# Joins of 16-bit halves in four pieces, late half copies over a head, one transfer and the unsplit stores at later steps

## The chip, the cores and the metric

One core of a Trainium2 chip runs the whole program. The metric is device microseconds of one execution; the engines that matter here are TensorE (PE), VectorE (DVE), ScalarE (ACT), GpSimd (POOL) and SyncE (SP), whose queue issues most transfers.

## The reference

Three layers follow one another: bucketed attention, a mixture of experts that sends each token to one of eight experts, and a gated feed-forward layer.

```python
# 2 batches, 8 heads, 768 tokens, head size 64
mask   = q_bucket[:, :, :, None] == k_bucket[:, :, None, :]
scores = np.where(mask, 0.125 * q @ k.T, -1e9)
x      = softmax(scores) @ v                       # to [1536, 512]
# 8 experts, 1536 tokens, width 512, hidden 1024
for e in range(8):
    m = e_idx == e                                 # argmax of x @ w_gate
    h = np.maximum(x[m] @ w1[e], 0)
    out[m] = gate_w[m, None] * eom[m, e, None] * (h @ w2[e])
# 1536 tokens, 512 -> 1536 -> 512
return ((out @ w_a) * (out @ w_b)) @ w_out
```

## The kernel before

The order of the instructions on each engine is the order of the code (a manual schedule); nothing reorders them.

**Precision.** Every fp32 operand of a matmul is split into a high part (ACT copies it to the narrower type) and a low part (DVE or POOL subtracts), and three matmuls replace one. `w_split` (L510, L511) does this for the weights of the experts, `x_parts` (L961, L962) for their inputs, `mm1` (L978, L979) for the hidden values `hl`.

**Attention**, 16 heads of six blocks of 128 queries, counted as (head, block). `smax` (L166, L167) ends with a small DVE instruction, `sb`, whose result ACT's exponential needs; PE then transposes the result (L188). The attention output `x_b` is kept in fp32 for the router and also written as two planes of 16-bit halves, `x_q` (POOL, `late_planes`, L224), because rows are sent to their expert's slots by POOL's indirect transfers (`scatter`, L454) and come back by a transposing transfer that takes 16-bit elements only. Expert 0's rows of batch 0 are fetched earlier by plain transfers and joined by `x0_join` (L409).

**Experts.** A step (e, f) is expert e with the hidden slice f of 128, 64 steps in all. In a step PE runs `mm1(e, f)` (12 matmuls) and then `mm2` of the step before (8 matmuls, L1005 and L1006); ACT and DVE make `hl` of the step, split the weights of two slots further on, and do what the schedule adds: `y_sum` at f = 0, `y_store` at f = 1 (high parts by ACT, L1029, low parts by DVE, L1030, unsplit copies by ACT, L1032). After each split SP issues the next load into the same buffer (`w_load`, four buffers for each half of a slot). `x_load(e)` is the transposing transfer of expert e's rows (L948, on SP), `x_join(e)` puts the two halves of its elements together again (POOL, L952), `x_parts` then splits them in two halves, i = 0 and 1. For expert 1 the load is issued ahead of step (0, 0), the join at (0, 5), the parts at (0, 6) and (0, 7). For a later expert the load is at f = 6 two experts ahead, the join at f = 3 and the parts at f = 4 and 6 of the expert before.

POOL also clears `y_h`, `y_l` and `y_w` (L851, four instructions for each), and at every third step from (1, 1) to (5, 2) sends one group of token numbers (`id_scatter`, L454). Ahead of each of these it reads one column of the step's `hl` (`spare`, L1091), so that it starts only after DVE has made `hl`. `hl` has three buffers: the value of step n + 3 can be written only when all readers of step n's are done.

Of the kernel before, what the change touches and what calls it, by code (L numbers as in the profile page):

```python
# [7 lines left out]
F32 = mybir.dt.float32  # L8
# [4 lines left out]
U16 = mybir.dt.uint16  # L13
# [11 lines left out]
C = 224  # L25
# [9 lines left out]
def attn_moe_kernel(ctx: ExitStack, tc: tile.TileContext, xin, cst, projd, wblk, wmoe, w2in, out):  # L35
    nc = tc.nc
    PE, ACT, DVE, POOL = nc.tensor, nc.scalar, nc.vector, nc.gpsimd
# [180 lines left out]
    def halves(ap):  # L218

        return ap.bitcast(U16).rearrange("p t (n a) -> p t a n", a=2)  # L220
# [5 lines left out]
    def late_planes(hh, t0=0, nt=6):  # L226
        to_planes(t0, nt, hh, halves(x_b)[:, t0:t0 + nt, :, hh * 64:(hh + 1) * 64])
# [177 lines left out]
    def x0_join():  # L405
        x0["g"] = xp.tile([128, 2, DM], F32, tag="x", name="x0")
        q = x0.pop("q").bitcast(U16).rearrange("p c (a n) -> p c a n", a=2)
        for c in range(2):
            POOL.tensor_copy(halves(x0["g"])[:, c], q[:, c])  # L409

    def x0_first(lo, hi):
        if lo == 0:
# [219 lines left out]
    with tc.manual_schedule():  # L632
# [80 lines left out]
        for g in range(NG):  # L713
# [75 lines left out]
            if h and h < L and t == 5 and K["avl"].count(5):  # L789
                o_evac(h - 1)  # L790
            side(2)
            if h == L - 2 and t > 2:
                late_planes(t - 3)
            for f in extra.get((h - L + 1, t), ()):
                f()
        o_out(L, qa)
# [48 lines left out]
        y_l = yp.tile([128, 4, N + C], F32R, name="y_l")  # L845
        y_w = yp.tile([128, 4, N + C], F32, name="y_w")

        def y_clear(*ys):
            for y in ys:
                for d in range(4):  # L850
                    POOL.memset(y[:, d], 0.0)  # L851

        y_clear(y_h.bitcast(F32))
        r2 = ctx_2.enter_context(tc.tile_pool(name="r2", bufs=2, reuse_waits="tile"))
        c2 = ctx_2.enter_context(tc.tile_pool(name="c2", bufs=2, reuse_waits="tile"))
        s2 = ctx_2.enter_context(tc.tile_pool(name="s2", bufs=4, reuse_waits="tile"))
# [90 lines left out]
            XG[e] = xg.tile([128, 8, C], U16, tag="xg", name="xg")  # L947
            after(nc.sync.dma_start(out=XG[e], in_=x_rows[e * C:(e + 1) * C], transpose=True), scat_x)  # L948

        def x_join(e):  # L950
            XI[e] = xg.tile([128, 4, C], F32, tag="xi", name="xi", bufs=1)
            POOL.tensor_copy(  # L952
                XI[e].bitcast(U16).rearrange("p d (n a) -> p a d n", a=2), XG.pop(e).rearrange("p (a d) n -> p a d n", a=2)
            )

        def x_parts(e, i):
# [68 lines left out]
        def y_store(e):  # L1025
            sl = bass.ds(o_regs[e], C)
            for d in range(4):
                y = YS[e, d]
                ACT.activation(y_h[:, d, sl], y, ACTF.Copy)  # L1029
                DVE.tensor_tensor(out=y_l[:, d, sl], in0=y, in1=y_h.bitcast(F32)[:, d, sl], op=ALU.subtract)  # L1030
            for d in range(4):
                ACT.activation(y_w[:, d, sl], YS.pop((e, d)), ACTF.Copy)  # L1032

# [28 lines left out]
            (7, 7): [ids_load, lambda: s_work(1, 1), lambda: s_work(1, 2)],  # L1062
        }
        steps = [(e, f) for e in range(E) for f in range(8)]
        x_load(1)
        for n, (e, f) in enumerate(steps):
            mm1(e, f)
            if n:
                mm2(*steps[n - 1])
            if f == 0 and e:  # L1070
                y_sum(e - 1)
            w_split(n + 2, 0)
            w_split(n + 1, 1)
            if f == 1 and e:
                y_store(e - 1)
            if e + 1 < E:
                if f == (3 if e else 5):
                    x_join(e + 1)
                for i in range(2):
                    if f == ((4, 6) if e else (6, 7))[i]:  # L1080
                        x_parts(e + 1, i)
            if (e, f) == (0, 5):
                y_clear(y_l.bitcast(F32), y_w)
            if f == 6 and e + 2 < E:
                x_load(e + 2)
            if e == E - 4 and f in (2, 4):
                w2_load(f // 2 - 1)
            for g in pre2.get((e, f), ()):
                g()
            if 9 <= n < 45 and n % 3 == 0:  # L1090
                POOL.tensor_copy(spare, HT[e, f].bitcast(F32)[:, 1, 0:1])  # L1091
                id_scatter(n // 3 - 3)
            if f == 0 and e or (e, f) == steps[-1]:
                offset_load(e - (f == 0))
# [363 lines left out]
```

## Time and profile before

| | |
|---|---|
| median of three runs | 737.4 us (736.58 to 739.29) |
| the profiled execution's own time | 735.29 us |
| its span, first to last instruction | 733.5 us |
| PE busy | 707.1 us, 96% of the span |
| DVE, ACT, POOL busy | 567.8, 447.4, 260.1 us |
| mean granted TensorE clock | 0.996 of full speed |

The span is the time from the first to the last instruction of the program on the profiled core; 1.8 us of the execution lie outside it. Busy shares are means over three stages: attention runs to about 260 us, the experts to about 441 us, the last layer to the end.

### The profile page before, as it was taken

To read this page: it belongs to the slowest core of one execution; us is meant where nothing else is said; L and a number is where in the kernel's file an instruction comes from. 1 tells how busy PE (TensorE), PEld (TensorE's weight loads), DVE (VectorE), ACT (ScalarE), POOL (GpSimd) and SP (SyncE) were. 2 spreads that over 40 slices of the span, in tenths; PEclk is the share of its full clock that TensorE was granted. 3 is DMA by queue.
4 is the path that set the end of the run, shared out by engine and by line. 5 is a ranking of instruction groups with operands and counts; after the bars stand their busy time and mean duration, and the time that the engine had idled before them with its cause. 6 is when DMAs were issued, how large, how long until landed. Compare 5 with 4: busy or idle time off the path is not lost.

```text
span 733.5 us, 13070 instructions
## 1 busy us (share of the span) xinstructions
PE 707.1 (96%) x4505; PEld 603.9 (82%) x4506; DVE 567.8 (77%) x1102; ACT 447.4 (61%) x962; POOL 260.1 (35%) x262
## 2 busy tenths in 40 slices
PE   7899999999999998899999999999999999999995
PEld 5676677667756688899899899999999999999994
DVE  6778777888787778788889887877777777777644
ACT  6878777777776447477778776576344454434320
POOL 3243343333545469232322103234322332233224
PEclk9999999999999999999999999999999999999999
DMA  7357351221301048579798740132212212121013
GB/s 254 106 216 262 102 171 59 88 87 59 135 15 62 15 131 267 172 224 222 209 281 240 238 139 30 57 109 71 80 53 64 87 58 86 35 82 59 0 51 126
DMA packets 53432, 88.01 MB, mean 120 GB/s; under 512 B 19872, under 2 KB 23280, under 8 KB 53360
## 3 DMA queue, kind: packets, MB, share of 16 engines
q1 hardware_dynamic: 50688, 80.61, 36.1%
q0 software_dynamic: 2304, 6.31, 2.3%
q8 instruction: 37, 0.61, 0.4%
q14 instruction: 35, 0.29, 0.1%
q10 hardware_dynamic: 368, 0.20, 0.1%
HBM read 69.65 MB, written 13.12 MB: 113 GB/s over the span
## 4 chain that ended last, share of the span: by engine, by line
PE 82%; DVE 5%; POOL 4%; ACT 3%; issue 2%; DMA 2%; ACTq 0%; SPq 0%; DVEq 0%; POOLq 0%
PE tp L188 9%; PE av L203 8%; PE y L1005 5%; PE s L160 4%; PE s L161 4%; PE aba L1227 4%; PE abb L1227 4%; PE abb L1229 3%; PE aba L1229 3%; PE abb L1228 3%; PE aba L1228 3%; PE q L1157 3%; PE q L1158 3%; PE q L1156 3%; PE h L967 3%; PE h L965 3%
## 5 line engine op out<-in xcount | busy, mean ns | idle before, releaser
L166 DVE TENSOR_REDUCE mm<-s 128x1 f32<-128x768 f32 x96 | 91.0, 948 | 25.2 <-PE s L161 24.7
L175 ACT ACTIVATE p<-s,sb 128x768 f32<-128x768 f32 x96 | 95.0, 989 | 24.1 <-DVE sb L167 23.0
L188 PEld LDWEIGHTS tp<-cs,p 128*128 128x128 f32 x576 | 64.1, 140 | 38.4 <-ACT p L175 25.1
L511 DVE TENSOR_TENSOR wl<-wr,wh 128x512 fp32r<-128x512 f32 x125 | 89.4, 755 | 6.1 <-ACT wh L510 1.3
L188 PE MATMUL tp<-cs,p 128*128 128x128 f32 x576 | 82.2, 279 | 6.2 <-ACT p L175 3.0
L938 POOL TENSOR_TENSOR pc<-t,pc 128x256 fp32r<-128x256 f32 x38 | 32.8, 867 | 152.8 <-ACT pc L937 138.1
L192 ACT ACTIVATE pt<-tp 128x384 f32<-128x384 f32 x143 | 65.0, 487 | 31.0 <-PE tp L188 31.0
L1005 PE MATMUL y<-hl,wh 128*128 128x448 f32 x224 | 75.8, 381 | 6.5 <-DVE hl L979 6.5
L510 ACT ACTIVATE wh<-wr 128x512 fp32r<-128x512 f32 x128 | 73.6, 623 | 2.7 <-DMA wr<-wmoe 2.7
L160 PE MATMUL s<-tk,tq 76*128 76x384 f32 x192 | 73.1, 381 | 0.5 <-DVE tq L137 0.5
L967 PE MATMUL h<-xh,wl 128*128 128x224 f32 x256 | 71.0, 278 | 1.5 <-DVE wl L511 1.5
L966 PE MATMUL h<-xl,wh 128*128 128x224 f32 x256 | 70.6, 276 | 0.8 <-DVE xl L962 0.5
L965 PE MATMUL h<-xh,wh 128*128 128x224 f32 x256 | 70.8, 276 | 0.2 <-ACT xh L444 0.2
L203 PE MATMUL av<-pt,v 128*64 128x384 f32 x360 | 68.0, 499 | 0.2 <-DVE r L238 0.2
L161 PE MATMUL s<-bk,bq 128*128 128x384 f32 x192 | 65.1, 339 | 0.0
L1006 PE MATMUL y<-hl,wl 128*128 128x224 f32 x224 | 59.9, 267 | 0.0
L1005 PEld LDWEIGHTS y<-hl,wh 128*128 128x128 f32 x224 | 42.6, 190 | 10.6 <-DVE hl L979 7.5
L967 PEld LDWEIGHTS h<-xh,wl 128*128 128x128 f32 x256 | 49.5, 193 | 1.7 <-DVE wl L511 1.7
L965 PEld LDWEIGHTS h<-xh,wh 128*128 128x128 f32 x256 | 49.3, 193 | 1.7 <-ACT xh L444 0.4
L966 PEld LDWEIGHTS h<-xl,wh 128*128 128x128 f32 x256 | 49.5, 193 | 1.2 <-DVE xl L962 0.7
L888 ACT ACTIVATE x<-r 128x512 uint8<-128x512 uint8 x36 | 28.5, 791 | 35.3 <-DVE x L885 35.3
L1117 ACT ACTIVATE gh<-p 128x384 fp32r<-128x384 f32 x21 | 11.0, 525 | 63.5 <-DVE p L1246 62.0
(260 smaller groups left out, 1940.5 us busy)
## 6 DMA issues: line engine op xcount, KB each, us to landing
wr<-wmoe SPq DMA_DIRECT2D x128, 256.0 KB
r<-w2in SPq DMA_DIRECT2D x36, 512.0 KB
x<-xin SPq DMA_DIRECT2D x30, 384.0 KB
xr<-zero SPq DMA_DIRECT2D x13, 512.0 KB
v<-xin SPq DMA_DIRECT2D x16, 192.0 KB
wb<-wblk SPq DMA_DIRECT2D x1, 640.0 KB
x<-xin SPq DMA_DIRECT2D x3, 192.0 KB
tq<-code SPq DMA_DIRECT2D x30, 18.0 KB
```

Of the source, the lines that this page charges most:

```text
L160: PE.matmul(p[:, c, :384], T[h, 0][:76, qs], T[h, 1][:76, sl], start=True, stop=False)
L161: PE.matmul(p[:, c, :384], B[h, 0][:, qs], B[h, 1][:, sl], start=False, stop=True)
L166: DVE.tensor_reduce(out=m[:, 1:2], in_=st[g][:, :, :384], axis=AX.XY, op=ALU.min)
L175: ACT.activation(p.rearrange("p (c n) -> p c n", c=2), st.pop(g)[:, :, :384], ACTF.Exp, scale=scl.pop(g), bias=nbs.pop(g), accum_out=sums[ ...
L188: PE.transpose(ps[:, j * 128:(j + 1) * 128], pt_[g][:, k * 128:(k + 1) * 128], ident)
L203: PE.matmul(av[h][c * 64:(c + 1) * 64, :384], v, PT[h][:, k, c * 384:(c + 1) * 384], start=(k == 0), stop=(k == NT - 1), skip_group_check= ...
L510: ACT.activation(h, r, ACTF.Copy)
L511: eng.tensor_tensor(out=l, in0=r, in1=h.bitcast(F32), op=ALU.subtract)
L965: PE.matmul(ps, wh, xh, start=first, stop=False)
L966: PE.matmul(ps, wh, xl, start=False, stop=False)
L967: PE.matmul(ps, wl, xh, start=False, stop=last)
L1005: PE.matmul(p, wh[:, w], hl, start=(f == 0), stop=False, skip_group_check=True)
```

## The change

`x0_join` and `x_join` are cut into four pieces each. The pieces of `x0_join` follow one another as before. Those of `x_join` go to the steps f = 1, 2, 4, 5 (for expert 1, two at (0, 4) and two at (0, 5)), and for expert 2 and the later ones each of them stands behind a `spare` copy of its step's `hl`. The three copies of `late_planes` that stood at blocks 3, 4 and 5 of head 13 go to blocks 1, 3 and 4 of head 14, each behind a one-column copy (`held`) of the newest `sb`. `x_load(1)` moves from ahead of step (0, 0) to (0, 3). Half of the clearing of `y_h` moves behind pieces of expert 1's join. The unsplit copies leave `y_store` and become `y_keep`, at f = 2 (at f = 4 for expert 0's result).

```diff
--- before.py
+++ after.py
@@ -406,7 +406,8 @@
         x0["g"] = xp.tile([128, 2, DM], F32, tag="x", name="x0")
         q = x0.pop("q").bitcast(U16).rearrange("p c (a n) -> p c a n", a=2)
         for c in range(2):
-            POOL.tensor_copy(halves(x0["g"])[:, c], q[:, c])
+            for w in (slice(0, 256), slice(256, 512)):
+                POOL.tensor_copy(halves(x0["g"])[:, c, :, w], q[:, c, :, w])
 
     def x0_first(lo, hi):
         if lo == 0:
@@ -789,8 +790,9 @@
             if h and h < L and t == 5 and K["avl"].count(5):
                 o_evac(h - 1)
             side(2)
-            if h == L - 2 and t > 2:
-                late_planes(t - 3)
+            if h == L - 1 and t in (1, 3, 4):
+                POOL.tensor_copy(held, last[0])
+                late_planes((1, 3, 4).index(t))
             for f in extra.get((h - L + 1, t), ()):
                 f()
         o_out(L, qa)
@@ -845,12 +847,11 @@
         y_l = yp.tile([128, 4, N + C], F32R, name="y_l")
         y_w = yp.tile([128, 4, N + C], F32, name="y_w")
 
-        def y_clear(*ys):
-            for y in ys:
-                for d in range(4):
-                    POOL.memset(y[:, d], 0.0)
-
-        y_clear(y_h.bitcast(F32))
+        def y_clear(y, ds=range(4)):
+            for d in ds:
+                POOL.memset(y[:, d], 0.0)
+
+        y_clear(y_h.bitcast(F32), (0, 1))
         r2 = ctx_2.enter_context(tc.tile_pool(name="r2", bufs=2, reuse_waits="tile"))
         c2 = ctx_2.enter_context(tc.tile_pool(name="c2", bufs=2, reuse_waits="tile"))
         s2 = ctx_2.enter_context(tc.tile_pool(name="s2", bufs=4, reuse_waits="tile"))
@@ -947,10 +948,12 @@
             XG[e] = xg.tile([128, 8, C], U16, tag="xg", name="xg")
             after(nc.sync.dma_start(out=XG[e], in_=x_rows[e * C:(e + 1) * C], transpose=True), scat_x)
 
-        def x_join(e):
-            XI[e] = xg.tile([128, 4, C], F32, tag="xi", name="xi", bufs=1)
+        def x_join(e, d):
+            if e not in XI:
+                XI[e] = xg.tile([128, 4, C], F32, tag="xi", name="xi", bufs=1)
             POOL.tensor_copy(
-                XI[e].bitcast(U16).rearrange("p d (n a) -> p a d n", a=2), XG.pop(e).rearrange("p (a d) n -> p a d n", a=2)
+                XI[e].bitcast(U16)[:, d].rearrange("p (n a) -> p a n", a=2),
+                XG[e].rearrange("p (a d) n -> p a d n", a=2)[:, :, d],
             )
 
         def x_parts(e, i):
@@ -1028,6 +1031,9 @@
                 y = YS[e, d]
                 ACT.activation(y_h[:, d, sl], y, ACTF.Copy)
                 DVE.tensor_tensor(out=y_l[:, d, sl], in0=y, in1=y_h.bitcast(F32)[:, d, sl], op=ALU.subtract)
+
+        def y_keep(e):
+            sl = bass.ds(o_regs[e], C)
             for d in range(4):
                 ACT.activation(y_w[:, d, sl], YS.pop((e, d)), ACTF.Copy)
 
@@ -1062,7 +1068,6 @@
             (7, 7): [ids_load, lambda: s_work(1, 1), lambda: s_work(1, 2)],
         }
         steps = [(e, f) for e in range(E) for f in range(8)]
-        x_load(1)
         for n, (e, f) in enumerate(steps):
             mm1(e, f)
             if n:
@@ -1073,14 +1078,25 @@
             w_split(n + 1, 1)
             if f == 1 and e:
                 y_store(e - 1)
+            if f == (4 if e == 1 else 2) and e:
+                y_keep(e - 1)
+            if (e, f) == (0, 3):
+                x_load(1)
             if e + 1 < E:
-                if f == (3 if e else 5):
-                    x_join(e + 1)
+                for d in range(4):
+                    if f == ((1, 2, 4, 5)[d] if e else 4 + d // 2):
+                        if e:
+                            POOL.tensor_copy(spare, HT[e, f].bitcast(F32)[:, 1, 0:1])
+                        x_join(e + 1, d)
                 for i in range(2):
                     if f == ((4, 6) if e else (6, 7))[i]:
                         x_parts(e + 1, i)
+            if (e, f) == (0, 4):
+                y_clear(y_h.bitcast(F32), (2,))
             if (e, f) == (0, 5):
-                y_clear(y_l.bitcast(F32), y_w)
+                y_clear(y_h.bitcast(F32), (3,))
+                y_clear(y_l.bitcast(F32))
+                y_clear(y_w)
             if f == 6 and e + 2 < E:
                 x_load(e + 2)
             if e == E - 4 and f in (2, 4):
```

On POOL, from the last row scatter of the router to expert 2's join (`xi` is the joined input, `xg` the transposed rows, `idtab` the token numbers), this stood in a row before:

```order
L454 DMA xr<-x_q,pos_i 3328x512 x6
L851 MEMSET y_h 128x1760 x4
L952 COPY xi<-xg 128x2x896
L851 MEMSET y_l 128x1760 x4
L851 MEMSET y_w 128x1760 x4
L1091 COPY spare<-hl 128x1
L454 DMA idtab<-tokc,cpos_i 1536x2
L952 COPY xi<-xg 128x2x896
```

and this stands there now:

```order
L455 DMA xr<-x_q,pos_i 3328x512 x6
L852 MEMSET y_h 128x1760 x2
L954 COPY xi<-xg 128x2x224 x2
L852 MEMSET y_h 128x1760
L954 COPY xi<-xg 128x2x224 x2
L852 MEMSET y_h 128x1760
L852 MEMSET y_l 128x1760 x4
L852 MEMSET y_w 128x1760 x4
L1089 COPY spare<-hl 128x1
L954 COPY xi<-xg 128x2x224
L1107 COPY spare<-hl 128x1
L455 DMA idtab<-tokc,cpos_i 1536x2
```

The whole join of expert 1 stood ahead of eight of the twelve clearing instructions; its first two pieces stand ahead of ten of them and the other two ahead of nine. The next expert's join has become pieces, each behind a `spare` copy of its own.

On SP, from the loads of the first weights (`wr`) on, this stood in a row before:

```order
L403 DMA x0q<-xr 128x512 x2
L501 DMA wr_2860<-wmoe 128x512
L501 DMA wr_2866<-wmoe 128x512
L501 DMA wr_3059<-wmoe 128x512
L948 DMA_TRANSPOSE xg<-xr 128x8x224
L501 DMA wr_3384<-wmoe 128x512
L501 DMA wr_3390<-wmoe 128x512
```

and this stands there now:

```order
L502 DMA wr_3385<-wmoe 128x512
L502 DMA wr_3391<-wmoe 128x512
L502 DMA wr_3425<-wmoe 128x512
L502 DMA wr_3431<-wmoe 128x512
L502 DMA wr_3468<-wmoe 128x512
L502 DMA wr_3474<-wmoe 128x512
L502 DMA wr_3524<-wmoe 128x512
L502 DMA wr_3530<-wmoe 128x512
L949 DMA_TRANSPOSE xg<-xr 128x8x224
L502 DMA wr_3567<-wmoe 128x512
```

The transposing transfer has moved behind eight weight loads, those of steps (0, 0) to (0, 3).

On ACT, at (7, 1) and (7, 2), where expert 6's result is stored, the end of the stores was this before:

```order
L1029 ISA
L1029 ACTIVATE y_h<-yt 128x224
L1032 ISA
L1032 ACTIVATE y_w<-yt 128x224
L1032 ISA
L1032 ACTIVATE y_w<-yt 128x224
L1032 ISA
L1032 ACTIVATE y_w<-yt 128x224
L1032 ISA
L1032 ACTIVATE y_w<-yt 128x224
L978 ACTIVATE hl<-h_5870 128x224
```

and is this now:

```order
L1032 ISA
L1032 ACTIVATE y_h<-yt 128x224
L981 ACTIVATE hl<-h_5916 128x224
L511 ACTIVATE wh_5944<-wr_5757 128x512
L511 ACTIVATE wh_5948<-wr_5763 128x512
L1038 ISA
L1038 ACTIVATE y_w<-yt 128x224
```

The next step's `hl` and weights have moved ahead of the four unsplit copies. On DVE and PE nothing changes its place.

## Rows read from the trace of the kernel before

**Rows 1.** PE's waits over the span: us in total, times, longest.

```profile
PE y L1005 <- DVE hl L979: 6.5, 5, 2.5
```

**Rows 2.** Engines by stretch: length; PE, PEld, DVE, ACT, POOL busy; clock; DMA; GB/s.

```profile
310.45:313.06 2.61, 2.61 (x22) 2.53 (x21) 1.87 (x5) 1.45 (x5) 1.28 (x2) 1.00 1.04 250
...
277.06:281.46 4.40, 2.86 (x22) 2.61 (x21) 4.33 (x8) 2.67 (x7) 4.40 (x4) 1.00 0.89 314
284.07:287.73 3.66, 3.12 (x22) 2.69 (x21) 2.83 (x10) 1.85 (x6) 3.66 (x4) 1.00 0.95 240
293.00:302.61 9.61, 7.08 (x43) 6.68 (x41) 7.17 (x12) 3.61 (x9) 3.03 (x3) 0.82 0.51 162
297.48:300.88 3.40, 3.40 (x17) 3.27 (x15) 2.20 (x5) 0.00 (x0) 0.00 (x0) 0.50 0.62 186
360.10:364.43 4.33, 2.87 (x23) 2.62 (x21) 4.33 (x8) 2.69 (x7) 1.79 (x1) 1.00 0.34 123
403.63:408.19 4.56, 2.85 (x22) 2.60 (x21) 4.56 (x9) 3.07 (x8) 1.16 (x1) 1.00 0.45 165
423.94:430.34 6.40, 6.08 (x50) 5.58 (x49) 4.59 (x12) 6.31 (x18) 0.00 (x0) 1.00 0.80 246
```

**Rows 3.** Timeline of DVE at (2, 1), where POOL joins nothing.

```profile
316.88 1.29 DVE L1030 TENSOR_TENSOR y_l<-yt,y_h 128x224 f32 x4
318.51 0.39 DVE L979 SCALAR_TENSOR_TENSOR hl<-h,hl 128x224 fp32r<-128x224 f32 x1 [0.34 <-ACT hl L978]
```

**Rows 4.** Timeline of DVE and POOL at step (1, 1): start, us, instruction.

```profile
293.01 3.06 DVE L1030 TENSOR_TENSOR y_l<-yt,y_h 128x224 f32 x1
...
292.39 1.26 POOL L454 DMA_INDIRECT idtab<-tokc,cpos_i  x1 [0.15 <-issue]
293.65 2.21 POOL L952 COPY xi<-xg 128x1792 uint16<-128x1792 uint16 x1
```

**Rows 5.** Timeline of SP and POOL around expert 7's transfer and join.

```profile
395.57 3.57 SPq L948 DMA_TRANSPOSE xg<-xr  x1
...
402.05 2.73 POOL L952 COPY xi<-xg 128x1792 uint16<-128x1792 uint16 x1
```

**Rows 6.** Timeline of ACT, SP and DVE at steps (0, 3) and (0, 4).

```profile
276.05 1.29 ACT L510 ACTIVATE wh<-wr 128x512 fp32r<-128x512 f32 x2 [2.17 <-DMA wr<-wmoe]
...
270.13 1.59 SPq L948 DMA_TRANSPOSE xg<-xr  x1
...
273.15 1.29 DVE L511 TENSOR_TENSOR wl<-wr,wh 128x512 fp32r<-128x512 f32 x2
276.71 2.81 DVE L511 TENSOR_TENSOR wl<-wr,wh 128x512 fp32r<-128x512 f32 x2 [1.30 <-ACT wh L510]
```

**Rows 7.** Timeline of ACT and PE at (7, 1) to (7, 2).

```profile
427.09 1.22 ACT L1032 ACTIVATE y_w<-yt 128x224 f32 x4
...
428.59 0.37 PE L994 MATMUL y<-hl,wh 128*128 128x224 f32 x1 [0.27 <-ACT hl L978]
```

**Rows 8.** Timeline of POOL, DVE and PE at the end of head 13.

```profile
212.58 2.35 POOL L224 COPY x_q<-x_b 128x768 uint16<-128x768 uint16 x3
...
213.22 1.73 DVE L167 SCALAR_TENSOR_TENSOR sb<-mm 128x2 f32<-128x2 f32 x1
...
216.20 0.33 PE L188 MATMUL tp<-cs,p 128*128 128x128 f32 x1 [1.13 <-DVE r L239]
```

**Rows 9.** POOL's column copies ahead of `id_scatter`: count, min/median/max ns, first and last start.

```profile
L1091 POOL COPY spare<-hl x12: 183/186/581, 291.7 to 383.4; 128x1 f32<-128x1 f32 x12
```

**Rows 10.** DMA packets that began between 270.13 and 273.9 us.

```profile
DMA packets 1854, 0.52 MB, mean 138 GB/s; under 512 B 1824, under 2 KB 1824, under 8 KB 1854
```

**Rows 11.** Timeline of POOL behind the last row scatter.

```profile
270.17 6.10 POOL L851 MEMSET y_h<- 128x1760 f32 x4 [2.07 <-DMA xr<-x_q,pos_i]
...
278.35 6.10 POOL L851 MEMSET y_l<- 128x1760 f32 x4
284.39 6.10 POOL L851 MEMSET y_w<- 128x1760 f32 x4
```

## Prediction

> **What bounds the kernel now.** I read the waits of PE first, since PE is busy for nearly the whole span. In the experts' stage its one repeated wait is for the low part of `hl` on DVE: five times, 6.5 us together [rows 1]. A wait of PE understates what is lost, so I took the stage step by step next, in the view of stretches [rows 2]. The first row there is an undisturbed step, 2.61 us from one `mm1` to the next. The reader should see how rarely a step is longer. Outside the first steps behind the router, which the change leaves alone, these are longer: (0, 6) with 4.40 us, 1.79 too much; (1, 0) with 3.66, 1.05 too much; (1, 3) and (1, 4) with 9.61 together, 4.39 too much; (4, 3) with 4.33, 1.72 too much; (6, 3) with 4.56, 1.95 too much. Steps (7, 2) and (7, 3) take 6.40 together, 1.18 more than two undisturbed steps; PE runs slightly longer matmuls in that expert, so I count 1.0. All this is 11.9 us. In the pair at 293 us half of the loss is the clock: PE's granted clock is 0.50 from 297.48 to 300.88 us, the level of 1.2 GHz, after PE had waited for `hl`; at half speed 3.4 us lose 1.7.
>
> Then I looked for what is late in each, in the timelines.
>
> At (1, 1) a `y_l` subtraction, 0.3 us in an undisturbed row of four [rows 3], takes 3.06 us, and it ends when POOL's whole join of 2.21 us ends [rows 4]. The next `hl` stands behind it on DVE, and PE waits for that. (4, 3) and (6, 3) are the same pattern; at (6, 1) the join takes 2.73 [rows 5]. The Trainium skill says the same in GPSIMD Engine Reference, Key points: POOL shares its SBUF interfaces with VectorE, and contends with VectorE instructions that have two SBUF inputs. The trace agrees, with 3.06 against 0.32. By that rule alone the time in which POOL may hold DVE rises, as an estimate, from 6 joins of 2.2 us to 24 pieces with their column copies, 19 us, and the gain at the joins would be in doubt.
>
> At (0, 4) ACT waits 2.17 us for weights [rows 6]. The transposing transfer stands at the head of SP's queue until the row scatters have landed, 270.13, and all weight loads behind it are late. DVE's pair of weight subtractions then takes 2.81 instead of 1.29 beside the join.
>
> At (7, 1) to (7, 2) ACT makes four unsplit copies, 1.22 us, ahead of `hl`, and PE waits for `hl` on ACT [rows 7]. At the end of head 13 three POOL copies in a row, 2.35 us, hold `sb` for 1.73, and PE idles 1.13 us soon after [rows 8].
>
> **The change part by part.**
>
> *Late copies, head 14.* Three copies of 0.78 us leave the place where they hold `sb` for 1.73 us; PE's wait of 1.13 goes. They come back in head 14 with three column copies, which I price like `spare`, 0.19 us each and 0.58 at most [rows 9]. A copy behind `sb` has most of a block's time until the next `sb`, but the last two meet other POOL work of that head. I charge 0.4 (bounds 0, if all fall between two `sb`, and 1.1, if one place waits as today): -0.7. The four pieces of `x0_join` run back to back as its two did; I count nothing, bounds -0.3 and +0.4, since DVE may get in between pieces or wait for all.
>
> *Transfer at (0, 3).* Weight loads no longer wait for the scatters, so the 2.17 us of ACT's wait and the longer subtraction go, and (0, 6) falls to 2.61: -1.8. The transfer itself is now behind the weight loads of step (0, 3), which wait for DVE's subtractions ending at 274.4 [rows 6]; with two issues it starts at about 274.9. Its 1,792 packets of 256 bytes had all begun 3.8 us after the issue [rows 10], which with a little for the landing gives 279.1; expert 7's, in a busier stretch, took 6.5 (395.57 to 402.05 [rows 5]), which gives 281.4. I take 279.1, since the rings are as empty here as at 270.
>
> *Expert 1's join and the clearing.* POOL now idles from 273.2 (two clears of 1.52, a quarter of 6.10 [rows 11]) until 279.1. A piece I put at 0.6 us: 0.55 is a quarter of 2.21, and 0.78 a third of the 2.35 of three larger copies [rows 8]. So: two pieces to 280.3, a clear to 281.8, two pieces to 283.0, a clear to 284.5, `y_l` to 290.6, `y_w` to 296.7; before, all ended at 290.5. PE, without the stall at (0, 6), begins (1, 0) at 277.06 + 2 x 2.61 = 282.3. Today the second parts cost step (1, 0) 1.05 us although the join was done by 278.35 [rows 11]; now ACT comes to them at about 282.4 and finds the last piece 0.6 us later: +0.65, step (1, 0) loses 1.7. (1, 1) begins at 286.6. Its `y_l` subtractions come near 290, when these clears are about done.
>
> *Steps (1, 1) to (1, 5).* The join that held `y_l` for 3.06 us is gone from (1, 1), and with it the slow clock: -4.4. What is late next is POOL. Its first `spare` reads (1, 1)'s `hl` only behind `y_w`, at 296.9; that buffer is wanted by `hl` of (1, 4), which ACT would write at 295.8 and PE needs at 298.3. ACT is 1.1 us late there and PE is not. Then come a piece, a `spare`, the scatter (1.26 us with 0.15 ahead of it [rows 4]), a `spare`, a piece: 299.9, when the first parts of expert 2 can start. ACT has `hl` of (1, 5) behind them, on DVE at 301.4; PE wants it at 300.9. I charge 0.8 in all: -3.6.
>
> *Steps (4, 3) and (6, 3).* A piece of 0.6 us behind `hl` holds one weight subtraction instead of 2.2 us on `y_l`. At (4, 3): -1.7. At (6, 1) the products of the last layer's weights on POOL stay: -1.5 of 1.95.
>
> *Unsplit copies.* For experts 1 to 6 four copies of 1.22 us leave (e, 1), the fullest step of ACT, for (e, 2). That frees `hl` of the next step by 1.2 us, and the loss at (7, 2) goes: -1.0. In the other experts it is not on PE's path: DVE waited for it 0.34 us [rows 3], PE not.
>
> What else moved past what: the clears and the scatter of (1, 1) wait behind the first join on POOL, and only `y_store`, `y_keep` and the list read at the end of the stage want them; SP's later loads wait for 1.6 us of the transfer's issue [rows 6] while their weights are two steps away.
>
> Sum: -0.7 - 1.8 + 0.65 - 3.6 - 1.7 - 1.5 - 1.0 = -9.65; I round to -9.4 for small new waits behind 24 gated pieces. From the profiled execution's 735.29 us this gives 725.9; the median of the three runs is 737.4, 2.1 higher, and the measured median should fall by the same amount: **728.0 us**.
>
> **The rivals.**
>
> *POOL's lateness takes the place of the join (1, 4).* For: 290.5 becomes 296.7 while PE is 5 us earlier, and each microsecond of a later landing counts at (1, 0) and again at (1, 5). Against: three `hl` buffers cover most of it. With 281.4 as the landing, 2.3 us come twice, and PE's wait at (1, 5) reaches the 2.5 us [rows 1] after which the clock was halved, 1.7 more: +6.3, 734.3 at most; a landing half-way gives 732. Chance 0.16.
>
> *The pieces hold DVE as often as they free it.* In (e, 0) and (e, 1) DVE works about 5.9 us against 5.2 of PE (two `hl` of 0.39, two pairs of weight subtractions of 1.29, four `y_l` of 1.29 together [rows 3, 6], and four sums that I put as long), so it ends 0.7 late; `hl` can be ready 0.8 after its matmuls and is wanted a step after them, which leaves 2.61 - 0.8 - 0.7 = 1.1 us. A piece and a column copy are 0.6 + 0.2 and fit; with the longest column copy, 0.58, they pass it by 0.1, and with that of a scatter as well by 0.7. At 0.6 in six experts the gain shrinks by 3.6: 731.6. Against: the gate lets `hl` through first. Chance 0.12. The Trainium skill's rule from GPSIMD Engine Reference speaks for this rival.
>
> *Nothing comes of it.* PE's matmuls may only wait elsewhere, as ACT and DVE stay as busy. Against: the undisturbed step [rows 2] shows PE's own rate with ACT busy 1.45 us and DVE 1.87 of its 2.61, so there is room for what moves. 736, chance 0.07.
>
> *Slower.* One mechanism: the transposing transfer lands late. Nothing else waits on SP's order here, but expert 1 cannot begin without it. The loss is 2 us for each, and two stretches of slow clock, 3.4; against -9.4 the kernel is slower by more than 3.7 from 13.1, that is a landing 4.85 us later than 279.1, at 284 us, 9 us after its issue. The longest in the rows is 6.5. Price at 284.2: 741.5. Chance 0.05.
>
> **How the numbers follow.** The likeliest case has 0.60 and its own range is 725 to 731: lower by 3 where the charges of 0.8, 0.65 and 0.4 vanish and pieces cost nothing, higher by 3 with pieces of 0.78 (0.7 more in the chain, twice) and 1.1 in head 14. The range 724.5 to 734.0 takes in the first two rivals and leaves out the last two and a little below, under 0.2. Under 0.5%, 3.7 us, this kernel's runs can't tell a change from none: the bound of faster is 733.7. That holds the likeliest case and nearly all of the first two rivals, 0.85; the same 0.10; slower 0.05.
>
> **What would show it.** Right: step (0, 6) at 2.61 with no wait of ACT for weights; no `y_l` or weight subtraction on DVE over 1.4 us; (1, 3) and (1, 4) without a stretch at clock 0.50; (4, 3), (6, 3) and (7, 3) near 2.65; head 13 without the wait of 1.13. The terms I trust least show at 279 to 301 us: POOL's start on expert 1's pieces, the end of `y_w`, and PE's waits at (1, 0) and (1, 5). If a slow clock appears there, the first rival holds. If `hl` of (e, 2) still ends PE's waits in several experts, the second does.

## The result, and the profile after

The changed kernel takes **727.57 us** (median of 4 runs, 727.09 to 728.39) where the kernel before took 737.91 (the three runs named at the start and a fourth, 736.58 to 739.29): a ratio of 0.9861, 95% interval 0.9839 to 0.9883, 10.3 us less. The profiled execution takes 728.01 us, its span is 726.3 us, its mean granted clock 0.995. By the two profiled executions only 7.3 us went; the other 3 us are taken up below.

The page's first part, busy time of each engine with its share of the span:

```profile
PE 706.5 (97%) x4505; PEld 604.2 (83%) x4506; DVE 558.9 (77%) x1102; ACT 448.2 (62%) x962; POOL 284.4 (39%) x312
```

POOL does 24 us more (pieces, their column copies), DVE 9 us less, since it is held for less time; PE does the same work in a shorter span. The view of stretches, for the steps that stood in [rows 2] (length; PE, PEld, DVE, ACT, POOL busy; clock; DMA; GB/s):

```profile
275.59:278.19 2.60, 2.60 (x22) 2.53 (x21) 2.31 (x8) 1.45 (x4) 0.60 (x1) 1.00 0.98 215
280.99:288.07 7.08, 4.83 (x20) 4.10 (x21) 5.25 (x12) 3.23 (x8) 7.08 (x7) 0.79 0.80 182
285.13:288.55 3.42, 3.42 (x16) 3.25 (x15) 1.69 (x6) 1.67 (x5) 3.42 (x3) 0.50 0.30 104
293.53:298.75 5.22, 5.22 (x42) 5.07 (x41) 4.02 (x10) 2.32 (x6) 5.06 (x7) 1.00 0.70 226
356.30:358.91 2.61, 2.61 (x23) 2.54 (x21) 2.35 (x7) 2.52 (x8) 2.26 (x3) 1.00 0.77 199
398.01:401.03 3.02, 2.87 (x23) 2.61 (x21) 3.02 (x8) 3.02 (x9) 1.50 (x3) 1.00 0.74 241
416.77:422.59 5.82, 5.82 (x51) 5.51 (x49) 4.46 (x11) 5.72 (x17) 0.00 (x0) 1.00 0.85 253
```

They are (0, 6), (1, 0), the stretch of slow clock, (1, 3) with (1, 4), (4, 3), (6, 3), and (7, 2) with (7, 3). Of the losses named there (6, 3) keeps 0.4 us and the last pair 0.6 (5.82 for two steps of 2.61); the others but one are gone. The exception is (1, 0): 7.08 where 3.66 stood. The slow clock of 297.5 us is gone too, but one of the same length now stands at 285.1 us. Its cause stands in the timelines of SP, POOL, ACT and PE:

```profile
264.44 8.06 SPq L502 DMA_DIRECT2D wr<-wmoe  x8
273.07 2.14 SPq L949 DMA_TRANSPOSE xg<-xr  x1
...
273.11 3.08 POOL L852 MEMSET y_h<- 128x1760 f32 x2 [5.10 <-DMA xr<-x_q,pos_i]
278.35 1.98 POOL L954 COPY xi<-xg 128x448 uint16<-128x448 uint16 x2 [2.16 <-DMA xg<-xr]
280.24 1.57 POOL L852 MEMSET y_h<- 128x1760 f32 x1
281.75 1.73 POOL L954 COPY xi<-xg 128x448 uint16<-128x448 uint16 x2
...
283.51 0.58 ACT L964 ACTIVATE xh<-xi 128x448 fp32r<-128x448 f32 x1 [1.29 <-POOL xi L954]
...
281.65 0.37 PE L969 MATMUL h<-xl,wh 128*128 128x224 f32 x1 [0.29 <-DVE xl L965]
284.14 0.37 PE L968 MATMUL h<-xh,wh 128*128 128x224 f32 x1 [1.67 <-ACT xh L964]
284.80 0.37 PE L969 MATMUL h<-xl,wh 128*128 128x224 f32 x1 [0.29 <-DVE xl L965]
```

The eight weight loads now go out while the row scatters are still under way, so the last scatter lands at about 273.1 us instead of 270.1 [rows 6, 11]: POOL, which waits for it, stands idle 5.10 us behind its issue instead of 2.07. In the four profiles with no load beside the scatters (before, runs 1, 8 and 12) this is 2.06 to 2.07, in the ten others 3.9 to 5.1. The transfer starts then, its rows are there at 278.35, and the pieces of the join take 0.99 and 0.87 us each, not 0.6. The last one ends at 283.48. PE had come to (1, 0) at 280.99 and waits three times.

### The profile page after: what moved, and what is told of

Read it like the earlier page. It is cut to its first block, busy times and chain, and to the rows that moved or that the text cites. A ratio compares the mean times of both kernels' runs of the same rounds, so it can differ in the third digit from the quotient of the medians.

```text
span 726.3 us, 13141 instructions
## 1 busy us (share of the span) xinstructions
PE 706.5 (97%) x4505; PEld 604.2 (83%) x4506; DVE 558.9 (77%) x1102; ACT 448.2 (62%) x962; POOL 284.4 (39%) x312
## 4 chain that ended last, share of the span: by engine, by line
PE 86%; DVE 5%; ACT 3%; DMA 2%; POOL 2%; issue 2%; SPq 0%; DVEq 0%; POOLq 0%; ACTq 0%
PE tp L188 9%; PE av L203 8%; PE y L1008 6%; PE s L160 4%; PE s L161 4%; PE aba L1243 4%; PE abb L1243 4%; PE abb L1245 3%; PE aba L1245 3%; PE abb L1244 3%; PE aba L1244 3%; PE q L1173 3%; PE h L969 3%; PE h L970 3%; PE q L1174 3%; PE h L968 3%
## 5 line engine op out<-in xcount | busy, mean ns | idle before, releaser
L512 DVE TENSOR_TENSOR wl<-wr,wh 128x512 fp32r<-128x512 f32 x125 | 83.5, 708 | 4.2 <-ACT wh L511 0.3
L939 POOL TENSOR_TENSOR pc<-s,pc 128x256 fp32r<-128x256 f32 x44 | 38.0, 874 | 33.0 <-ACT pc L938 31.4
```

The costliest lines, as they stand in the source:

```text
L512: eng.tensor_tensor(out=l, in0=r, in1=h.bitcast(F32), op=ALU.subtract)
```

## Experiments

One number for the first expert's transfer runs through them: by how much the steps exceed 2.61 us each, once from the start of (0, 3) to that of (1, 0), five steps, and once from there to (1, 7), seven steps. It is worked out from the starts of each step's first matmul in the profiled execution: after the change 280.99 - 267.77 - 5 x 2.61 = 0.17.

| kernel | median us | ratio to before | (0, 3) to (1, 0) | (1, 0) to (1, 7) | sum |
|---|---|---|---|---|---|
| before, the profile shown | 737.4 | | 3.16 | 5.49 | 8.7 |
| after | 727.57 | 0.9861 | 0.17 | 4.91 | 5.1 |
| 1 before again | 738.29 | 1.0005 | 6.24 | 3.88 | 10.1 |
| 2 before, transfer at (0, 3) | 736.83 | 0.9993 | 2.17 | 6.56 | 8.7 |
| 3 after, whole join, gated | 730.26 | 0.9902 | 2.17 | 5.98 | 8.2 |
| 4 after, pieces, ungated | 731.11 | 0.9922 | 1.74 | 4.71 | 6.5 |
| 5 after, transfer at (0, 1) | 727.05 | 0.9873 | 1.33 | 2.53 | 3.9 |
| 6 as 5, pieces first | 726.33 | 0.9856 | 1.20 | 2.49 | 3.7 |
| 7 after, pieces first | 728.81 | 0.9888 | 2.48 | 5.25 | 7.7 |
| 8 before, late copies only | 737.29 | 1.0003 | 4.68 | 5.46 | 10.1 |
| 9 as 6, three clears ahead | 726.32 | 0.9843 | 0.02 | 2.94 | 3.0 |
| 10 as 9, transfer at (0, 2) | 726.28 | 0.9849 | -0.02 | 3.11 | 3.1 |
| 11 before, transfer at (0, 1) | 735.69 | 0.9970 | 0.50 | 6.43 | 6.9 |
| 12 before, unsplit copies later | 737.01 | 0.9992 | 6.10 | 3.86 | 10.0 |

Runs 1 to 4, 5 to 8 and 9 to 12 each share their runs of before (medians 737.98, 737.02 and 738.00), so across these groups the ratios compare, not the medians; runs 9 to 12 are from another chip than 1 to 8. The last three columns are of one execution each.

### 1 and 2. The kernel before again, and with the transfer alone moved

Run 1 has no edit. Run 2:

```diff
-        x_load(1)
         for n, (e, f) in enumerate(steps):
...
+            if (e, f) == (0, 3):
+                x_load(1)
```

> The kernel before, unchanged, to see which of its losses belong to every execution. Its profile lost 0.85 and 0.52 us at steps (0, 3) and (0, 4), where ACT stood still from 265.6 to 269.1 us, and these are gone in the changed kernel, which the prediction did not foresee. Theory: the stop comes with the transfer that holds SP's queue at its head, so it stands here again (3.4 to 3.5 and 3.1 us). Rival: it was a stray of one execution, and the two steps take 2.61 here. Both: (0, 6) 4.4, (1, 3) and (1, 4) together 9 to 10 us, (4, 3) 4.3, (6, 3) 4.5; time 737.9, ratio 1.000.

> The kernel before with x_load(1) at (0, 3) and nothing else. Theory: the weights come in time, so (0, 6) falls from 4.40 to 2.61, and (0, 3) and (0, 4) too if their loss hangs on the transfer: -1.8 to -3.2. The whole join, behind all four clears of y_h, ends near 281.5, and the second parts come 1 to 2 us late, so step (1, 0) takes 6 to 7.5 us with a stretch of slow clock in place of 3.66; (1, 3) and (1, 4) keep their 9 to 10. Sum 0 to +1: 737 to 739. Rival: the late load costs expert 1 nothing beyond today's 1.05, and the whole gains 2 to 3: 735.

Measured: 1.0005 [0.9988, 1.0022] and 0.9993 [0.9973, 1.0012]. Stretches of run 1, then of run 2:

```profile
277.79:284.59 6.80, 5.10 (x20) 4.74 (x21) 6.38 (x12) 4.00 (x8) 6.80 (x5) 0.62 0.97 336
279.40:286.20 6.80, 6.23 (x26) 6.06 (x27) 5.41 (x13) 2.88 (x6) 6.80 (x6) 0.50 0.87 299
296.90:304.91 8.01, 5.49 (x43) 5.15 (x41) 7.17 (x12) 3.59 (x9) 3.03 (x3) 1.00 0.48 145
```

```profile
276.49:279.09 2.60, 2.60 (x22) 2.53 (x21) 2.31 (x8) 1.45 (x4) 2.29 (x2) 1.00 1.30 127
279.09:283.33 4.24, 2.77 (x23) 2.44 (x21) 1.16 (x3) 0.96 (x3) 2.86 (x2) 1.00 1.00 332
283.33:289.58 6.25, 5.29 (x21) 4.49 (x21) 4.29 (x12) 3.12 (x8) 6.25 (x5) 0.62 0.74 204
```

Two things follow. First, the profile from which I predicted was not a usual execution. In run 1 step (0, 6) takes 6.80, not 4.40, with 6.8 us at half clock from 279.4; (1, 3) with (1, 4) takes 8.01, not 9.61. Runs 8 and 12, which share the early transfer, agree in the sum: 10.1, 10.1 and 10.0 in the last column against 8.7. Nor did ACT's stop at (0, 3) come again in run 1, both steps took 2.61, so the transfer at the queue's head does not bring it about. Second, the transfer at (0, 3) alone frees (0, 6), 2.60, and gives all of it back at (0, 7) and (1, 0), where the rows come late.

### 3 and 4. The cut without its smallness, and without its gate

Run 3 joins expert 2 and later ones in one instruction again, at f = 3, but behind a `spare`; run 4 keeps the pieces and drops the `spare` ahead of each.

```diff
# run 3; in x_join, d may be a slice there (not shown)
-                    if f == ((1, 2, 4, 5)[d] if e else 4 + d // 2):
+                    if not e and f == 4 + d // 2:
+                        x_join(e + 1, d)
+                if e and f == 3:
+                    POOL.tensor_copy(spare, HT[e, f].bitcast(F32)[:, 1, 0:1])
+                    x_join(e + 1)
# run 4
-                        if e:
-                            POOL.tensor_copy(spare, HT[e, f].bitcast(F32)[:, 1, 0:1])
```

> The changed kernel, but from expert 2 on the join is whole again (2.2 to 2.7 us, one instruction) and stands at f = 3 behind one copy of that step's hl, as the pieces do. Theory of place: the loss came from the step at which the hold fell, (e, 1), DVE's fullest, and ahead of hl; behind hl of (e, 3) DVE ends 1.3 us late of 1.8 that it has, so no step from (1, 3) on is longer than in the changed kernel: 727 to 728.5. Theory of size: a hold of 2.2 us on DVE stops PE wherever it falls: steps (e, 4) lose 0.5 to 1.7 each, six times, +3 to +10: 731 to 738.

> The changed kernel without the copy of hl ahead of each piece of x_join from expert 2 on, so POOL runs a piece as soon as it is free. Theory of place: at (4, 1) and at (6, 1) two pieces, 1.4 us, fall on y_l again and steps (4, 3) and (6, 3) lose 0.3 to 1.7 each: +0.5 to +3, 728 to 730.5. Theory of size: pieces of 0.7 us are short enough anywhere, (4, 3) stays at 2.61 and the time at 727.6.

Measured: 0.9902 [0.9884, 0.9919] and 0.9922 [0.9901, 0.9943]. Run 3, POOL and DVE at (6, 3) and (6, 4), and the stretches (4, 3), (6, 3), (6, 5):

```profile
404.87 0.55 POOL L1091 COPY spare<-hl 128x1 f32<-128x1 f32 x1 [4.29 <-DVE hl L983]
405.36 2.71 POOL L954 COPY xi<-xg 128x1792 uint16<-128x1792 uint16 x1
...
405.89 2.46 DVE L886 TENSOR_SCALAR x<-t 128x512 uint32<-128x512 uint32 x1
...
360.27:362.88 2.61, 2.61 (x22) 2.54 (x21) 1.88 (x5) 2.51 (x8) 0.09 (x1) 1.00 0.98 230
402.09:404.70 2.61, 2.61 (x22) 2.54 (x21) 2.61 (x8) 2.61 (x9) 0.00 (x0) 1.00 0.69 221
407.31:411.20 3.89, 2.87 (x22) 2.62 (x21) 2.72 (x5) 2.82 (x7) 0.76 (x1) 1.00 0.59 178
```

Run 4, POOL, DVE and PE at (6, 1) to (6, 3), and the stretches (4, 3) and (6, 3):

```profile
395.84 1.72 POOL L939 TENSOR_TENSOR pc<-t,pc 128x256 fp32r<-128x256 f32 x2 [12.22 <-ACT pc L938]
397.50 2.99 POOL L954 COPY xi<-xg 128x448 uint16<-128x448 uint16 x3
...
396.86 2.30 DVE L512 TENSOR_TENSOR wl<-wr,wh 128x512 fp32r<-128x512 f32 x2
399.09 2.62 DVE L1033 TENSOR_TENSOR y_l<-yt,y_h 128x224 f32 x4
...
402.07 0.47 PE L1008 MATMUL y<-hl,wh 128*128 128x448 f32 x1 [1.50 <-DVE hl L982]
...
357.36:359.97 2.61, 2.61 (x23) 2.54 (x21) 2.61 (x5) 2.52 (x8) 2.47 (x3) 1.00 0.59 213
399.07:403.42 4.35, 2.85 (x23) 2.61 (x21) 4.35 (x9) 3.08 (x9) 2.15 (x3) 1.00 0.54 186
```

Gate and cut each suffice at (4, 3). At (6, 3) the gate is needed: without it three pieces, late behind the products of the last layer's weights, run back to back and hold DVE like a whole join: two groups of 1.29 us take 2.30 and 2.62, and the step takes 4.35, nearly as before the change (4.56). With the gate even a whole join leaves (6, 3) at 2.61, but it holds another DVE instruction, `x` of the last layer's weights, for 2.46 us (0.41 at the same place after the change). ACT waits for that ahead of the next `hl`, and (6, 5) pays 1.28. The rest of what run 3 loses in the experts lies mostly at (0, 3) to (1, 1): its transfer was asked for at 275.9 and the rows came at 281.8, 3.4 us later than in the profile after. Runs 4 and 7 lie between (rows at 280.3 and 280.8). So the medians of runs 3 and 4 are not the price of cut and gate alone: these stalls of the first expert are in them. The profile of run 3 (732.69) is also the slowest of its four executions, that of run 4 (729.65) the fastest. Neither run fell where a theory put it: 730.26 lies between the two ranges given for run 3, with a loss at (6, 5) that the theory of place had excluded, and 731.11 above both given for run 4, with none of the loss expected at (4, 3).

### 5, 6 and 7. An earlier transfer, and all pieces first

```diff
# runs 5 and 6
-            if (e, f) == (0, 3):
+            if (e, f) == (0, 1):
                 x_load(1)
# runs 6 and 7
-                    if f == ((1, 2, 4, 5)[d] if e else 4 + d // 2):
+                    if f == ((1, 2, 4, 5)[d] if e else 4):
```

> The changed kernel with expert 1's transposing transfer two steps earlier, at (0, 1): behind four weight loads instead of eight, ahead of the others. My theory: the stage's largest loss that is left, 4.9 us at (0, 7) to (1, 1) (slow clock included), is there because the rows land late; they were asked for at 273.1, 274.9 and 275.9 us in the three runs that had the transfer at (0, 3). At (0, 1) it stands at SP's head until the last row scatter has landed, about 271.5 with four loads fewer beside the scatters, so the rows land near 277 and the four pieces with one clear between them end near 282, 1.5 us earlier than after the change. The waits at (1, 0) go down by that much each and the stretch of slow clock goes: 724 to 726 us by the median. The loads now behind the transfer are first wanted at about 279, so (0, 6) stays at 2.61. Rival: four loads behind the transfer are late again, as all eight were before the change, and (0, 5) to (0, 7) lose 1.8 or more: 727 to 729.

> As the run with the transfer at (0, 1), and all four pieces of expert 1's join at (0, 4), ahead of the second half of the clearing of y_h. The last piece ends another 1.5 us earlier, near 280.5. My theory: nothing is then left to wait for at (1, 0), whose loss falls under 1 us, 723 to 725 by the median. Rival: PE's wait there is not for the pieces but for ACT and DVE, which split x behind their own work at (0, 6) and (0, 7): the same time as with the transfer moved alone.

> The changed kernel, transfer at (0, 3) as there, with all four pieces of expert 1's join at (0, 4), ahead of the second half of the clearing of y_h. The third and fourth piece start 1.55 us earlier. If the clear that stands between the pieces is the cause of the wait for xh at (1, 0), 1.67 us, that wait nearly goes, and perhaps the slow clock behind it: 724.5 to 727. If the landing of the transfer alone decides, the first parts wait as long as before and only the second ones gain: 727 to 728.

Measured: 0.9873 [0.9832, 0.9915], 0.9856 [0.9820, 0.9892] and 0.9888 [0.9852, 0.9925]. Run 5, SP, then step (1, 0); below it (1, 0) of run 7, its slow clock, and POOL's four pieces in run 7 and in run 6:

```profile
265.07 2.43 SPq L502 DMA_DIRECT2D wr<-wmoe  x4
273.07 1.60 SPq L949 DMA_TRANSPOSE xg<-xr  x1
...
282.79:286.87 4.08, 3.12 (x23) 2.68 (x21) 3.19 (x11) 2.33 (x7) 4.08 (x4) 1.00 1.15 198
```

```profile
282.76:289.37 6.61, 5.02 (x20) 4.38 (x21) 4.65 (x12) 3.12 (x8) 6.61 (x6) 0.68 0.84 232
285.20:292.00 6.80, 6.19 (x26) 6.01 (x27) 4.45 (x14) 2.82 (x7) 6.80 (x5) 0.50 0.41 104
...
280.81 2.49 POOL L954 COPY xi<-xg 128x448 uint16<-128x448 uint16 x4 [5.85 <-DMA xg<-xr]
...
277.95 3.30 POOL L954 COPY xi<-xg 128x448 uint16<-128x448 uint16 x4 [2.33 <-DMA xg<-xr]
```

Among these runs the landing decides, not the clear between the pieces: with the late transfer, pieces first still lose 4.0 at (1, 0), and with the early one (1, 0) falls to 4.08 and 4.31 and there is no slow clock in either. Runs 6 and 7 are the clean pair: they differ in the transfer's place alone, ACT stops in both (3.4 us), PE comes to (1, 0) at 282.44 and 282.76, and the rows are there at 277.95 and 280.81. Against the profile after the change runs 5 and 6 show less: their rows came only 0.2 and 0.4 us earlier, and PE came 1.8 and 1.4 later, for the most part through ACT's stop. My figure for the scatters was wrong (they landed at about 273, not 271.5). The medians, 727.05 and 726.33, lie 0.5 and 1.2 below that of the change, less than I gave, and by the ratios, 0.9873 and 0.9856 beside 0.9861, neither run can be told from it; run 7, at 728.81, came out above both of its ranges. What replaces the loss is the first rival of the prediction in small: in run 5 ACT stands idle 2.51 us ahead of `hl` of (1, 4), until a `spare` behind the clears is through, and (1, 6) takes 3.52.

### 8 and 12. The late copies alone, the unsplit copies alone

Run 8 is the kernel before with `late_planes` in head 14 and `x0_join` in pieces, as in the change's diff; run 12 has `y_keep` alone.

> The kernel before with the late half copies spread over head 14, each behind its column copy, and the join of expert 0's rows in pieces; nothing else. Theory: the wait of 1.13 us of PE near 216 us goes, another of about 0.7 comes near 241, and the first mm1 of the experts starts 0.4 to 0.6 us earlier; the median falls by 0.5, within what the runs can tell from nothing. Rival: the copies in head 14 hold DVE more than that, no gain or a loss of 0.5.

> The kernel before with the unsplit copies as y_keep at (e, 2), (1, 4) for expert 0's, and nothing else. Theory: (7, 2) and (7, 3) together lose 0.6 less, and (4, 3), (6, 3) and (1, 3) lose what they lose today: a median 0.6 lower, hardly to be told from nothing. Rival: at (1, 1) and the like the four copies of 1.22 us on ACT were part of what made hl late, and the losses of (1, 3), (4, 3) and (6, 3) shrink by 0.5 or more each: 2 to 3 us faster.

Measured: 1.0003 [0.9986, 1.0021] and 0.9992 [0.9974, 1.0010]. In run 8 PE's wait at 216 us is gone and none at 241 took its place (in the profile after the change one of 0.69 did, at 240.93), but the first `mm1` of the experts starts between 259.4 and 261.5 us in the fourteen profiles, whichever place the copies have (259.41 in run 8, 259.50 in run 10, 261.34 in run 3): 0.7 us can't be read out of that. Run 12, (7, 2) with (7, 3), and (4, 3):

```profile
425.99:431.80 5.81, 5.81 (x50) 5.51 (x49) 4.45 (x11) 5.72 (x17) 0.00 (x0) 1.00 0.79 256
362.16:366.48 4.32, 2.87 (x23) 2.61 (x21) 4.32 (x7) 2.89 (x8) 1.78 (x1) 1.00 0.29 100
```

The first is as after the change, the second as before it: the copies' place is worth 0.6 us, in the last expert alone.

### 9, 10 and 11. Three clears ahead, the transfer at (0, 2), and the transfer at (0, 1) alone

```diff
# runs 9 and 10, on top of run 6; run 10 with (0, 2) for (0, 1)
-        y_clear(y_h.bitcast(F32), (0, 1))
+        y_clear(y_h.bitcast(F32), (0, 1, 2))
...
-            if (e, f) == (0, 4):
-                y_clear(y_h.bitcast(F32), (2,))
# run 11, on top of the kernel before
-        x_load(1)
+            if (e, f) == (0, 1):
+                x_load(1)
```

> The changed kernel with expert 1's transfer at (0, 1), all four pieces of its join at (0, 4), and three of the four clears of y_h (instead of two) ahead of them, in the 2.3 us in which POOL idled until the rows landed. My theory: with the transfer early, what is left at (1, 3) to (1, 6), 0.7 to 1.0 us, is POOL's lateness: ACT's hl of (1, 4) waited 2.2 to 2.5 us for a spare copy behind y_w's clears, which ended at 296.3 and 296.7. One clear of 1.5 us earlier ends them at 294.8, hl of (1, 4) is on time, and (1, 6) falls to 2.61: 725 to 726 by the median, and no loss of (1, 0) beyond the 1.7 of the run without the third clear. Rival: the pieces start 1.5 us later because the third clear is in their way: (1, 0) loses 1 more, 727.

> As the run with three clears ahead, but the transfer at (0, 2), behind six weight loads. With it at (0, 1) SP stood at the transfer from 267.5 to 273.1 and ACT then waited up to 1.20 us for weights at (0, 7); behind six loads it would start at about the same time, since the sixth ends near 272 and the last row scatter lands near then. Theory: ACT's wait for weights goes and (1, 0) loses 1.0 or less, 724.5 to 725.5. Rival: the two loads delay the scatters and the transfer, (1, 0) is back at 5 and more: 727 to 728.

> The kernel before with one edit: expert 1's transfer at (0, 1) instead of ahead of (0, 0). With the transfer at (0, 3) this edit alone was worth nothing, as what (0, 6) gained was given back at (1, 0). Theory: at (0, 1) it keeps the gain of 1.8 at (0, 6), gives back at most 1 at (1, 0), and leaves the 4.4 at (1, 3) and (1, 4) as they are, since the whole join at (1, 1) still stands behind the clears: 735.5 to 736.5 by the median. Rival: the losses at (1, 3) and (1, 4) are themselves due to weights that come late in a row, and fall as well: 731 to 733.

Measured: 0.9843 [0.9808, 0.9879], 0.9849 [0.9811, 0.9886] and 0.9970 [0.9948, 0.9991]. ACT at 279.54 us, between `hl` of (0, 6) and of (0, 7), in run 9; SP, POOL's pieces, (1, 0) and ACT at (1, 4) in run 10:

```profile
279.54 0.63 ACT L511 ACTIVATE wh<-wr 128x512 fp32r<-128x512 f32 x1 [1.30 <-DMA wr<-wmoe]
```

```profile
271.96 1.60 SPq L949 DMA_TRANSPOSE xg<-xr  x1
...
276.96 3.76 POOL L954 COPY xi<-xg 128x448 uint16<-128x448 uint16 x4 [0.39 <-DMA xg<-xr]
...
279.73:284.33 4.60, 3.39 (x23) 2.77 (x21) 3.77 (x12) 2.52 (x7) 4.60 (x5) 1.00 1.12 319
...
295.19 0.36 ACT L981 ACTIVATE hl<-h 128x224 fp32r<-128x224 f32 x1 [2.58 <-POOL spare L1105]
```

In run 9 the lateness at (1, 4) nearly goes, (1, 6) 2.77, as expected, but (1, 0) is at 5.22: ACT waits for weights that stood behind the transfer, and the rows, at 278.79, come 0.8 us later than in run 6. In run 10 that wait is gone; (1, 0) loses 1.99, more than I gave, and (1, 6) loses 0.94, since PE came to (1, 4) 2.5 us earlier than in run 9 and POOL's clears ended only 1.0 earlier. Both end near 3 us in the table's last column, 2 us better than the changed kernel, and their medians are 1.3 us lower, still above what I gave. The intervals overlap with that of the change, so the time alone does not tell them apart. In both, the rows come as long ahead of PE at (1, 0) as after the change (2.8 us; 2.6 there), so here it is not the landing that differs but the pieces in a row: the last one ends 0.2 and 1.0 us behind PE's arrival instead of 2.5, and the clock stays at 1.00. Run 11 has the median that I gave and is 2.3 us faster than before, but by other steps: (1, 0) loses 3.5, with a slow clock, and (1, 3) loses 2.5, not 4.4. The rest of the gain must come from pieces, gates and the order of the clearing; that follows by difference, no run has them alone.

## Why the prediction was right, and where its terms were not

The forecast was 728.0 and 727.57 came. The sum was nearly right; several terms were not, and that their errors cancelled is luck. By the profiled executions, in us:

| term | forecast | profile |
|---|---|---|
| late copies, head 14 (start of the first `mm1`) | -0.7 | -0.1 |
| (0, 3), (0, 4) | 0 | -1.4 |
| transfer: (0, 5) to (0, 7) | -1.8 | -1.6 |
| expert 1's join: (1, 0), (1, 1) | +0.65 | +3.7 |
| (1, 3) to (1, 6) | -3.6 | -4.2 |
| (4, 3) | -1.7 | -1.7 |
| (6, 3) | -1.5 | -1.55 |
| (7, 2), (7, 3) | -1.0 | -0.6 |
| the rest, the last layer in it | +0.25 | +0.2 |
| sum | -9.4 | -7.3 |

**Steps (4, 3) and (6, 3).** Right in size and in cause, as runs 3 and 4 show. A piece of the next join does meet DVE, for instance at (6, 1) after the change, POOL's timeline and then DVE's:

```profile
396.44 0.65 POOL L1089 COPY spare<-hl 128x1 f32<-128x1 f32 x1
397.03 1.18 POOL L954 COPY xi<-xg 128x448 uint16<-128x448 uint16 x1
...
395.80 1.85 DVE L512 TENSOR_TENSOR wl<-wr,wh 128x512 fp32r<-128x512 f32 x2
397.57 1.73 DVE L1033 TENSOR_TENSOR y_l<-yt,y_h 128x224 f32 x4
```

DVE loses 1.0 us (1.85 and 1.73 against 1.29 each [rows 3, 6]) and POOL as much (1.83 us for a piece and a column that take 0.69 and 0.18 at 297.4 and 298.0), and (6, 3) loses 0.4. The second rival's 0.6 in each of six experts did not come. The Trainium skill, in SBUF — State Buffer, section SBUF: two separate sides, calls the pair of ports that VectorE and GpSimd share an exclusive lock: the one that starts first has it for its whole instruction. The rows agree in what a hold costs: one subtraction took 3.06 us and ended 0.2 us behind the whole join (296.07 against 295.86 [rows 4]), a piece costs half a microsecond. They do not show who came first: by its record that subtraction began at 293.01, ahead of the join's 293.65, while POOL issued an indirect transfer.

**Step (1, 0).** This is the term that failed: "finds the last piece 0.6 us later: +0.65". The loss grew by 3.4 us there and 0.2 at (1, 1). Three figures were off. Beside DVE a piece took 0.9 to 1.0 us; my 0.6 came from rows in which POOL had not been held up, and holds in run 7, where DVE stood idle beside most of it (2.49 us for four). PE came 1.3 us earlier than I had it, since (0, 3) and (0, 4) lost nothing, so it met the same late rows with more to wait. And the clock fell to 0.50 for 3.4 us after these waits, 1.7 us that stood in the first rival alone.

The landing itself I had nearly right, 278.4 for 279.1, but for the wrong reason: the scatters, slowed by weight loads beside them, set the start of the transfer at 273.07, 1.8 us earlier than I had it, and the rows took 5.3 us instead of 4.2. Where ACT stood still (next point) the weight loads did, as I had argued, at 274.4 to 275.9 in runs 2, 3, 4 and 7, and the rows came 5.4 to 6.5 us later, close to the 281.4 of the long bound. The reading behind that bound was no landing, though: ahead of expert 7's join POOL was busy with products of the last layer's weights from 400.39 to 402.11 us, so 6.5 only bounds it from above. Run 6 against run 7 shows that late rows cause the loss: rows 2.9 us earlier take away 2.3 us at (1, 0) and the slow clock. Runs 9 and 10 take away 1.9 and 2.5 us and the slow clock by the pieces in a row; how much of the 3.4 is the landing's and how much the clear's between the pieces is not settled.

**Steps (0, 3) and (0, 4).** Not foreseen, and not from the change. ACT stood idle 3.0 to 3.5 us ahead of the third `hl` in the profile of before and in those of runs 3 to 7, 2.3 in run 2, 1.6 and 1.95 in runs 1 and 8, and 1.2, the least, after the change and in runs 9 to 12. The kernel before shows both, 3.53 in the profile shown and 1.60 in run 1. The rows are of run 5 and then of the kernel after:

```profile
269.62 0.36 ACT L981 ACTIVATE hl<-h 128x224 fp32r<-128x224 f32 x1 [3.50 <-PE y L1009]
```

```profile
266.70 0.36 ACT L981 ACTIVATE hl<-h 128x224 fp32r<-128x224 f32 x1 [1.21 <-PE h L970]
```

Where it stops for 3 us or more, PE loses 1.2 to 1.4. The records name no event that would have held it, so the cause stays open.

**Steps (1, 3) to (1, 6).** The mechanism was right: the whole join is gone from (1, 1) and POOL's lateness comes next. My clears ended at 296.7 and they end at 297.05; ACT stands idle 1.69 us ahead of `hl` of (1, 4), where 1.22 was enough a step before, so it is half a microsecond late and not 1.1, and PE loses 0.2, not 0.8.

**From the profile to the median.** "The measured median should fall by the same amount" was wrong, and it saved the number: the profiles alone would have led from 737.4 to 730.1. The profile fell by 7.3, the median by 10.3. Of the difference 2.6 us are there because the profiled execution of before, 735.29, lies below the four other runs of that kernel, and 0.4 because that of after lies above its median. Three other profiles with the transfer ahead of (0, 0) lose 1.3 to 1.5 us more at (0, 3) to (1, 7), each with 6.8 us at half clock there where the one shown has 3.4. In that one (0, 6) loses 1.8; in the others (0, 5) to (0, 7) lose 4.7 to 6.2. The change takes that away too, which is about half of the 3 us; the rest is not placed. Run 8 shows one more place where executions differ: a third stretch at half clock, 3.4 us from 407.3, and 1.6 us more at (6, 3) and (6, 4).

**The last expert** was mis-sized, 0.6 for 1.0; **head 14** can't be told, as run 8 shows.

**The signs.** (0, 6) at 2.60 with no wait for weights, no `y_l` or weight subtraction over 1.25 us, (1, 3) and (1, 4) at full clock, (4, 3) at 2.61 and head 13 without its wait all came. (6, 3) at 3.02 and (7, 3) at 2.93 are not near 2.65. A slow clock between 279 and 301 us was to mean that the first rival holds, and it came, at 285.13. Half of that rival held: with late rows (1, 0) lost 3.4 us more. Its second half, the same loss again at (1, 5), did not come; that step takes 2.61.

## What to carry to other kernels

A transfer that waits at the head of a queue costs twice, by what it holds up behind it and by how late its own data come; where it stands best lies between (here anywhere from (0, 1) to (0, 3), by times that the runs do not tell apart), and the step that consumes its data shows how far it may move. A copy on POOL that shares ports with DVE costs least when it is short and starts behind the instruction that must not wait: the gated whole join of run 3 still cost 1.28 us at another place, and the ungated pieces of run 4 cost as much as a whole join where they ran back to back. Before terms are priced from one profile, see where its time stands among the runs: one that is 2 us faster than the median may lack a stall that the median has, as here.

## Of the hardware, unexpected

Clears on POOL do not hold DVE: after the change four `y_l` subtractions take 1.29 us at 293.11 while POOL clears `y_w` from 290.93 to 297.05, where one piece beside them at (6, 1) costs 0.44. An instruction with one tensor input is held as well: `x` in run 3, 2.46 us. POOL's copies are slowed as much as DVE's instructions: 0.69 us alone, up to 1.18 beside two-input subtractions. The granted clock does not follow from the sum of PE's waits: in run 9 PE waited 2.1 us in two waits at (1, 0) and the clock stayed at 1.00; in run 7, 1.7 us in two waits up to 283.8 were followed by 6.8 us at 0.50.
